# Decode-step transformer block on one core: the first w_mod load issued as 16 rows and 112 rows

## The chip, the cores and the metric

The kernel runs on one core of one Trainium2 chip. The metric is the device time of one execution in microseconds. TensorE (PE), VectorE (DVE), ScalarE (ACT) and GpSimd (POOL) compute; SyncE (SP) issues all DMA transfers of this kernel from one queue, and 16 DMA engines carry them out.

## What is computed

Two sequences with one new token each (B = 2, D = 512) go through an adaptive-layernorm block. The condition c gives six vectors per sequence, which scale, shift and gate an attention over the last 4096 positions of a cache (32 query heads on 8 key/value heads of 128) and a SiLU feed-forward of width 1792. All is float32.

```python
mod = (_silu(c) @ w_mod).reshape(c.shape[0], 6, 1, -1)
sa, ca, ga, sb, cb, gb = (mod[:, i] for i in range(6))
h = _layernorm(x) * (1 + ca) + sa
x = x + ga * attention(h, k_cache[:, :, -4096:], v_cache[:, :, -4096:], wq, wo)
h = _layernorm(x) * (1 + cb) + sb
x = x + gb * (_silu(h @ w1) @ w2)
```

Almost all bytes are read once: 64 MB of keys and values, and the weights w_mod (512 x 3072), wq (512 x 4096), wo (4096 x 512), w1 and w2.

## The kernel before, in words

Every large input is loaded in pieces of 128 rows into a ring of eight buffers of 128 x 4096 floats (`ring`, L55; `stream`, L69). A piece may be loaded when the piece eight places before it in the ring has been used. All loads are issued by SyncE in program order: `load_rows` (L72) for w_mod and wq, `load_k` and `load_v` (L77, L84) for the cache, `load_runs` (L91) for wo, w1 and w2. Each DMA signals its end on one of eight semaphores, taken in turn.

The program begins with the loads. L103 loads rows 0 to 127 of w_mod (`wm0`, 128 x 3072), then L107 loads c and x, each in two DMAs of small pieces, into `c_ch` and `x_ch`, which VectorE has cleared (L102). L111 loads the three other pieces of w_mod (`wm1` to `wm3`), L112 the four of wq. The loads of k and v follow in the loop over the heads.

Meanwhile VectorE and GpSimd build constants (L115 to L195): an identity and small selection matrices. VectorE transposes c (L235), its SiLU is made (L203 to L206, L238), and TensorE multiplies it with the pieces of w_mod (L246, L249). From the result and the normalised x comes `hq_T` (L263), the input of the q matmuls over the four pieces of wq (L285). The loop (L448) then takes one key/value head after the other: transposes of the keys on VectorE (L337), scores (L349), softmax, and the weighted sum of the values (L423). The tail multiplies with wo (L550, L561), does the second layernorm and the feed-forward (L595, L631, L643), and stores the output (L656).

The order of the instructions on each engine is a scheduler's, except in the loop and the tail, where `inorder` keeps the program's order. The operations of the beginning, those of VectorE among them, have no such mark.

Of the kernel before, what the change touches and what calls it, by code (L numbers as in the profile page):

```python
# [13 lines left out]
P = 128  # L14
B, D = 2, 512
# [8 lines left out]
def adaln_block(  # L24
# [21 lines left out]
    nc = tc.nc  # L46
# [22 lines left out]
    def stream(name):  # L69
        return ring.tile([P, 4096], F32, tag="st", name=name)  # L70

    def load_rows(name, w, k, width):  # L72
        t = stream(f"{name}{k}")[:, :width]
        nc.sync.dma_start(t, w[k * P : (k + 1) * P, :])
        return t
# [24 lines left out]
    x_sp, x_ch, c_ch = const([P, P], "x_sp"), const([P, P], "x_ch"), const([P, P], "c_ch")  # L100
    for t in (c_ch, x_ch, x_sp):
        nc.vector.memset(t, 0.0)  # L102
    wm = [load_rows("wm", w_mod, 0, 6 * D)]  # L103
    rows8 = lambda t: t.rearrange("(ab r) m -> ab r m", r=16)[:, 0, :]
    for t, src in ((c_ch, c), (x_ch, x2)):
        for b in range(B):
# [577 lines left out]
```

## Time and profile before

| | us |
|---|---|
| three runs: median (lowest, highest) | 237.36 (237.23, 237.38) |
| the profiled execution: its own time | 236.89 |
| the profiled execution: span from first to last instruction | 235.0 |

The profile describes the one profiled execution; times in it count from the span's start. A page gives busy times per engine, DMA queues and the chain of work that ended last. A window row gives, for a stretch A:B, its length, then for PE, PEld (weight loads), DVE, ACT and POOL the busy time in us and the number of instructions, then the granted TensorE clock, the mean busy share of the 16 DMA engines and the GB/s that they moved; a packet is counted where it starts, so a share can be above 1. A timeline row gives start, duration, engine (SPq is SyncE's issuing of DMAs), line, operation, tiles and, in brackets, how long the engine had been idle and what ended that. A row of the chain of waits gives start, duration and what the end was waiting for.

### The profile page before, as it was taken

How to read it: one execution, taken by the hardware profiler on the slowest of the kernel's cores; microseconds unless marked ns; L12 is line 12 of the kernel's file. 1: busy time of each engine (PE TensorE's matmuls, PEld its weight loads, DVE VectorE, ACT ScalarE, POOL GpSimd, SP SyncE). 2: the span in 40 equal slices, each digit the busy share in tenths (PEclk: the TensorE clock that was granted, in tenths of full speed). 3: DMA queues.
4: the chain of work that ended last, by engine and by line, in shares of the span. 5: the costliest groups of instructions: out<-in, count | busy, mean ns of one | idle time of the engine just before them, and what ended most of it. 6: DMA issues, size and time to landing. Idle time of an engine off the chain costs nothing.

```text
span 235.0 us, 2644 instructions
## 1 busy us (share of the span) xinstructions
PE 146.5 (62%) x1094; PEld 45.9 (20%) x1094; DVE 114.6 (49%) x176; ACT 25.4 (11%) x56; POOL 10.3 (4%) x30
## 2 busy tenths in 40 slices
PE   0086546367187577667549519626743967788993
PEld 0032101101011121121112102111211222335332
DVE  0634000793694792693892792595298050002130
ACT  2200000100300200200200200200020021003210
POOL 8600000100000000000000000000000000000000
PEclk9999975759869997999976967965985799999999
DMA  6999999999999999999999999999999999999991
GB/s 253 426 438 427 427 438 427 424 439 427 429 441 424 427 438 427 429 438 424 429 435 429 427 432 432 432 429 432 428 429 429 429 432 429 432 426 422 421 412 56
DMA packets 7603, 97.69 MB, mean 416 GB/s; under 512 B 920, under 2 KB 936, under 8 KB 1576
## 3 DMA queue, kind: packets, MB, share of 16 engines
q1 hardware_dynamic: 7592, 97.54, 97.5%
q8 instruction: 8, 0.13, 0.2%
q14 instruction: 3, 0.02, 0.0%
HBM read 97.53 MB, written 0.00 MB: 415 GB/s over the span
## 4 chain that ended last, share of the span: by engine, by line
DMA 64%; DVE 22%; PE 10%; ACT 2%; issue 1%; SPq 1%; DVEq 0%
DVE kT L337 16%; DMA wo<-in_A_wo_dram 14%; DMA k<-in_A_k_cache_dram 14%; DMA v<-in_A_v_cache_dram 13%; DMA wq<-in_A_wq_dram 13%; DMA w<-in_B_w_dram 7%; PE s L349 5%; DMA wm<-in_w_mod_dram 3%; DVE zp L395 2%; PE o L423 2%; PE q L285 1%; DVE xp L393 1%; ACT pr L381 1%; DVE mx L359 1%; ACT L381 1%
## 5 line engine op out<-in xcount | busy, mean ns | idle before, releaser
L337 DVE STREAM_TRANSPOSE kT<-k 128x1024 f32<-128x1024 f32 x64 | 73.7, 1210 | 1.6 <-DMA k<-in_A_k_cache_dram 1.6
L349 PE MATMUL s<-kT,qbd 128*32 128x512 f32 x256 | 44.5, 670 | 11.2 <-DVE kT L337 11.1
L423 PE MATMUL o<-v,ptb 128*32 128x512 f32 x256 | 38.5, 730 | 19.8 <-DMA v<-in_A_v_cache_dram 19.3
L359 DVE TENSOR_REDUCE mx<-s 128x1 f32<-128x512 f32 x8 | 5.5, 691 | 40.1 <-PE s L349 40.1
L349 PEld LDWEIGHTS s<-kT,qbd 128*32 128x32 f32 x256 | 11.1, 126 | 45.8 <-issue 24.1
L285 PE MATMUL q<-wq,hq_T 128*32 128x512 f32 x64 | 11.2, 836 | 10.1 <-DMA wq<-in_A_wq_dram 10.1
L423 PEld LDWEIGHTS o<-v,ptb 128*32 128x32 f32 x256 | 8.1, 124 | 35.8 <-issue 33.1
L402 PE MATMUL pT<-zp,id 128*32 128x256 f32 x64 | 5.6, 418 | 13.9 <-DVE zp L395 13.9
L379 ACT COPY bias<-bp 128x1 f32<-128x1 f32 x8 | 1.3, 159 | 111.9 <-PE bp L377 111.9
L537 PE MATMUL junk<-selh,id 128*32 128x256 f32 x46 | 11.3, 380 | 0.0
L294 DVE STREAM_TRANSPOSE qT<-q 128x512 f32<-128x512 f32 x2 | 1.4, 718 | 18.6 <-PE q L285 18.3
L395 DVE TENSOR_TENSOR zp<-xp,group 128x1024 f32<-128x1024 f32 x8 | 9.8, 1225 | 0.2
L393 DVE STREAM_TRANSPOSE xp<-pr 128x512 f32<-128x512 f32 x8 | 5.6, 701 | 4.4 <-ACT pr L381 4.4
L217 PE MATMUL mean_a<-mv_a,avg 128*128 128x1 f32 x2 | 0.6, 362 | 10.6 <-DVE mv_a L214 10.6
L361 PE MATMUL mT<-ident,mx 128*1 128x128 f32 x16 | 3.0, 270 | 6.4 <-DVE mx L359 6.4
L550 PE MATMUL acc_o<-wo,oTn 128*32 128x512 f32 x48 | 5.8, 598 | 1.9 <-DMA wo<-in_A_wo_dram 1.6
L537 PEld LDWEIGHTS junk<-selh,id 128*32 128x32 f32 x46 | 5.0, 110 | 6.7 <-issue 3.5
L438 PE MATMUL o_all<-ob,selh 128*64 128x128 f32 x64 | 5.7, 304 | 0.8 <-ACT ob L432 0.8
L270 DVE STREAM_TRANSPOSE xT<-x_sp 128x128 f32<-128x128 f32 x1 | 0.4, 403 | 11.8 <-DMA x_sp<-in_A_x_dram 11.8
L432 ACT COPY ob<-o 128x512 f32<-128x512 f32 x8 | 4.7, 585 | 10.3 <-PE o L423 10.3
L285 PEld LDWEIGHTS q<-wq,hq_T 128*32 128x32 f32 x64 | 2.1, 128 | 18.8 <-DMA wq<-in_A_wq_dram 12.5
L249 PE MATMUL m_sp<-wm,scT 128*32 128x512 f32 x32 | 5.7, 796 | 0.0
(132 smaller groups left out, 95.0 us busy)
## 6 DMA issues: line engine op xcount, KB each, us to landing
k<-in_A_k_cache_dram SPq DMA_DIRECT2D x16, 2048.0 KB, 30.2
v<-in_A_v_cache_dram SPq DMA_DIRECT2D x16, 2048.0 KB, 31.5
wq<-in_A_wq_dram SPq DMA_DIRECT2D x4, 2048.0 KB
wo<-in_A_wo_dram SPq DMA_DIRECT2D x4, 2048.0 KB, 32.3
wm<-in_w_mod_dram SPq DMA_DIRECT2D x4, 1536.0 KB, 10.2
w<-in_B_w_dram SPq DMA_DIRECT2D x2, 1024.0 KB, 23.2
w<-in_B_w_dram SPq DMA_DIRECT2D x1, 1792.0 KB
w<-in_B_w_dram SPq DMA_DIRECT2D x2, 896.0 KB
```

The lines of the kernel that those rows point to most:

```text
L249: nc.tensor.matmul(m_sp[r, :], scT[:, k, :], cd[:, g], start=(k == 0), stop=(k == 3))
L285: nc.tensor.matmul(q_ps[n][32 * g : 32 * g + 32, :], hq_T[:, k, :], wv[:, n, g], start=(k == 0), stop=(k == 3),)
L337: inorder(nc.vector.transpose(kT[h, b][:, :, 8 * n4 : 8 * n4 + 8, :].rearrange("p j n k -> p n j k"), kt[h, b][:, n4 * 1024 : (n4 + 1) * 1 ...
L349: inorder(nc.tensor.matmul(s_ps[h][r : r + 32, :], qbd[h // 4][:, h % 4, b, j, :], kT[h, b][:, j, 16 * c : 16 * c + 16, :], start=(j == 0) ...
L359: inorder(nc.vector.tensor_reduce(mx, s_ps[h], axis=AX.X, op=ALU.max))
L393: inorder(nc.vector.transpose(xp, pr[h]))
L395: inorder(nc.vector.tensor_mul(zp, xp[:, None, :, 0:16].to_broadcast([P, 4, 16, 16]), group[:, :, None, None].to_broadcast([P, 4, 16, 16]),))
L402: inorder(nc.tensor.matmul(tp[32 * i : 32 * i + 32, :], id4, zp.rearrange("p a s x -> p (a s) x")[:, :, 4 * i : 4 * i + 4], start=True, st ...
L423: inorder(nc.tensor.matmul(o_ps[h][32 * c : 32 * c + 32, :], ptb[h % 2][:, 256 * b + 32 * w : 256 * b + 32 * w + 32], vt[h, b][:, 512 * w ...
L438: inorder(nc.tensor.matmul(o_all[r : r + 64, :], selh[:, m, HQ - G - G * h : 3 * HQ - G - G * h], o_sb[h][:, m * DH : (m + 1) * DH], start ...
L537: inorder(nc.tensor.matmul(junk[0:32, :256], id4, selh.rearrange("p m y -> p (m y)")[:, :256], start=True, stop=True,))
L550: inorder(nc.tensor.matmul(acc[32 * g : 32 * g + 32, :], oTn[:, q, :], wot[q // 8][:, q % 8, :], start=(q < 4), stop=(q >= 20),))
```

## The change

The load of rows 0 to 127 of w_mod is issued as two DMAs into the same buffer, rows 0 to 15 first and rows 16 to 127 second. Both are ahead of the loads of c and x, as the one DMA was. All else in the source is the same; lines behind the change have numbers that are higher by four.

```diff
-    wm = [load_rows("wm", w_mod, 0, 6 * D)]
+
+    wm0 = stream("wm0")[:, : 6 * D]
+    for p0, p1 in ((0, 16), (16, P)):
+        nc.sync.dma_start(wm0[p0:p1, :], w_mod[p0:p1, :])
+    wm = [wm0]
     rows8 = lambda t: t.rearrange("(ab r) m -> ab r m", r=16)[:, 0, :]
     for t, src in ((c_ch, c), (x_ch, x2)):
         for b in range(B):
```

In the built program SyncE has one DMA more, and two VectorE instructions, the transpose of c (L235) and the first step of its SiLU (L203), stand behind the set-up operations on the identity, which they preceded. The instructions of the other engines stand as they did.

## The prediction

> **What bounds the kernel now.** I read the page first, for the share of each engine and the row of the DMA queue:
>
> ```profile
> span 235.0 us, 2644 instructions
> PE 146.5 (62%) x1094; PEld 45.9 (20%) x1094; DVE 114.6 (49%) x176; ACT 25.4 (11%) x56; POOL 10.3 (4%) x30
> ...
> q1 hardware_dynamic: 7592, 97.54, 97.5%
> ```
>
> No computing engine is busy for more than 62% of the span, while the packets of the one queue that SyncE feeds fill 97.5% of it. To see whether that queue ever runs dry, and where it starts and stops, I then cut the span into windows (the last two columns are the mean busy share of the 16 DMA engines, and GB/s):
>
> ```profile
> 0.00:1.50 1.50, 0.00 (x0) 0.00 (x0) 0.50 (x5) 0.77 (x1) 0.89 (x7) 1.00 0.00 0
> 1.50:2.00 0.50, 0.00 (x0) 0.00 (x0) 0.00 (x0) 0.50 (x1) 0.50 (x2) 1.00 1.55 270
> 2.00:2.50 0.50, 0.00 (x0) 0.00 (x0) 0.00 (x0) 0.02 (x1) 0.50 (x4) 1.00 0.20 49
> 2.50:3.00 0.50, 0.00 (x0) 0.00 (x0) 0.00 (x0) 0.00 (x0) 0.50 (x3) 1.00 0.63 221
> 3.00:3.50 0.50, 0.00 (x0) 0.00 (x0) 0.00 (x0) 0.00 (x0) 0.50 (x2) 1.00 0.98 418
> ...
> 4.00:228.00 224.00, 143.02 (x1034) 44.18 (x1035) 113.52 (x169) 23.55 (x54) 6.91 (x16) 0.86 1.01 430
> ...
> 228.50:229.00 0.50, 0.50 (x4) 0.22 (x2) 0.00 (x0) 0.38 (x1) 0.00 (x0) 1.00 0.92 369
> 229.00:229.50 0.50, 0.48 (x7) 0.17 (x9) 0.00 (x0) 0.21 (x1) 0.00 (x0) 1.00 0.77 311
> ```
>
> From 4 to 228 us the DMA engines are busy all the time (1.01; packets are counted where they start) at 430 GB/s. So the kernel is one stream of bytes: nothing before 1.5 us, a ragged first 1.5 us, 224 us at full rate, and a tail. The chain of waits, in order of time, shows what follows the last byte:
>
> ```profile
> 0.73 6.16 DMA wm<-in_w_mod_dram
> ...
> 213.97 16.51 DMA w<-in_B_w_dram
> 230.48 0.04 issue
> 230.53 1.10 PE acc_y L643 x24
> ```
>
> After the last weights land at 230.48 us comes a fixed end of 4.5 us up to the span's 235.0. Hence the rule for this kernel: a microsecond lost or won at the head of the stream is lost or won at the end, because no later gap takes it up. The change touches just that head.
>
> For later use: 430 GB/s over 16 engines that are busy 1.01 of the time is 26.6 GB/s for each, so one row of w_mod (3072 floats, 12,288 bytes) takes an engine 0.46 us.
>
> **The change part by part.** The profiled execution took 236.89 us, 1.89 outside its span; the median shown is 237.36, 0.47 more. I work out a difference from the profiled execution and add it to the median.
>
> *One more DMA on SyncE's queue.* The rows of that queue:
>
> ```profile
> 0.73 0.40 SPq L74 DMA_DIRECT2D wm<-in_w_mod_dram  x1
> 1.19 1.29 SPq L107 DMA_DIRECT2D c_ch<-in_c_dram  x2
> 2.53 1.09 SPq L107 DMA_DIRECT2D x_ch<-in_A_x_dram  x2
> 3.65 1.40 SPq L74 DMA_DIRECT2D wm<-in_w_mod_dram  x3
> 6.91 1.81 SPq L74 DMA_DIRECT2D wq<-in_A_wq_dram  x4
> 16.14 5.23 SPq L79 DMA_DIRECT2D k<-in_A_k_cache_dram  x4
> ...
> 181.60 0.58 SPq L474 DMA_DIRECT2D x_sp<-in_A_x_dram  x1
> 7.09 0.31 DVE L235 STREAM_TRANSPOSE cT<-c_ch 128x128 f32<-128x128 f32 x1 [5.75 <-DMA c_ch<-in_c_dram]
> ```
>
> A load of wm costs SyncE 0.40 us at the front and 1.40 / 3 = 0.47 later. The second part therefore pushes the loads of c, of x and of wm1 to wm3 back by some 0.45 us. In time this costs nothing: wm1 would be issued at 4.1 instead of 3.65, while the bytes of wm0 keep the engines occupied until its landing at 0.73 + 6.16 = 6.89 us, and c, which stands in line behind wm0, is seen by VectorE at 7.09. Without that cover the price would be 0.45 us. Each part has a semaphore of its own out of eight that go round, so behind it every user shifts by one: the load of wm3 now waits for the 16 rows and that of wq0 for the 112 (in the kernel before, wq0 waits for the whole of wm0: hence the jump to 6.91). The 16 rows are long there when SyncE comes to wm3 at about 5 us, and wq0 is no later than now. Behind them every load waits for the eighth before it, as now. Costed at nothing; if the 16 rows landed past 5 us, only wm3 and the wq loads queue behind the wait, with two loads of 3.7 us in stock.
>
> *VectorE's order.* In the order of instructions the transpose L235 and L203 that follows it now stand behind the nine set-up operations of which these are the first and the last but one:
>
> ```profile
> 7.32 0.33 DVE L118 TENSOR_REDUCE id<-ident 128x32 f32<-128x128 f32 x1
> ...
> 9.72 0.17 DVE L156 COPY selh<-id 128x32 f32<-128x32 f32 x1
> ...
> 13.29 1.08 PE L246 MATMUL m_ch<-wm,scT 128*32 128x256 f32 x8 [0.86 <-DVE scT L238]
> ...
> 22.99 1.93 PE L285 MATMUL q<-wq,hq_T 128*32 128x512 f32 x16 [2.02 <-DMA wq<-in_A_wq_dram]
> ...
> 39.01 1.94 PE L285 MATMUL q<-wq,hq_T 128*32 128x512 f32 x8 [2.06 <-DMA wq<-in_A_wq_dram]
> ```
>
> So the set-up from 7.32 to 9.8 us is done while VectorE waits for c, and the first modulation matmul may start up to 2.5 us before 13.29. That gain is hidden: the q matmuls wait for wq anyway, from 22.99 to 39.01, and the k loads that wm's freed buffers allow (16.14) stand in a queue that is full. Nothing for the time; it is cover against a later wm0.
>
> *How the stream starts.* The 0.1 us windows show the first packets:
>
> ```profile
> 1.60:1.70 0.10, 0.00 (x0) 0.00 (x0) 0.00 (x0) 0.10 (x1) 0.10 (x2) 1.00 0.00 0
> 1.70:1.80 0.10, 0.00 (x0) 0.00 (x0) 0.00 (x0) 0.10 (x1) 0.10 (x1) 1.00 3.48 614
> ```
>
> They start at 1.7. By 3.0 us, 0.5 x (270 + 49 + 221) = 270 KB have been started, where 430 GB/s from 1.7 on would have made 559. So at most 289 KB / 430 = 0.67 us is there to be won at the head. An earlier first packet isn't to be had: the load of x_sp, eight rows, took SyncE 0.58 us to issue, no less than 128 rows did. Part of the 0.67 can come if a short first load sets all engines going together, where now 11 packets (135 KB) start in 1.5 to 2.0 us and 2 in the next half microsecond. But the second part is issued 0.45 us later than those rows are now. Bounds: -0.67 to +0.45. I take half the gain, **-0.33 us**.
>
> *The 16 rows themselves.* All big loads here have 128 rows; none shows what a 16-row load does, whose rows lie in 16 neighbouring partitions. From below: all 16 engines abreast, one row each, 0.46 us, no loss. From above: each row behind the other, 16 x 0.46 = 7.4 us. The nearest row is the first window: 0.5 us x 16 x 1.55 = 12.4 engine-us on 11 packets, 1.13 us each, so that even rows spread over 128 partitions take 2.4 times their price at the start. Neighbours can only be worse: I take the geometric middle of the bounds, four row times, 1.85 us, a loss of 1.85 - 0.46 = **+1.39 us**.
>
> [...]
>
> *The 112 rows.* Each engine has 7 rows where it had 8. If they are dealt out as evenly as 128 rows are, no loss; if all go as the 16 do, 7 x 1.39 = +9.7 us. Since the 112 span nearly the partitions of the 128 rows, which run at full rate, I stay near that end with one row time, **+0.46 us**, and up to three (+1.39) for the range.
>
> **Sum:** -0.33 + 1.39 + 0.46 = +1.52 us, 237.36 + 1.52 = **238.9 us**; on the profiled execution 238.4.
>
> **The rivals.** About 0.2% (0.47 us, from 236.89 to 237.83) is what a measurement can tell from no change.
>
> *The rows do not obstruct each other.* Then only the start counts: half its gain, or the second part late by up to 0.45 us: 237.0 to 237.8, likeliest **237.2**. For it: the stream runs at 430 GB/s however the 16 engines' rows fall. Against: that is shown for 128 rows alone.
>
> *Faster: a clean start.* With no obstruction and no late second part the ragged head closes, -0.67 us: **236.7**. It decides if more than 0.47 of the 0.67 us comes back, that is if by 3.0 us over 470 KB have been started in place of 270. For it: the hole at 2.0 to 2.5 us (49 GB/s). Against: the later second part, and that first packets of 1.13 us look slow on their own account.
>
> *The 112 rows obstruct throughout:* +1.39 + 9.7 - 0.33, about **248**.
>
> *It doesn't change the head,* since both parts queue on the same engines at once: this is the first rival's time.
>
> **How the numbers follow.** Forecast (obstruction at the head) 0.47, no obstruction 0.35, clean start 0.14, obstruction throughout 0.04. From the last and the forecast comes slower, 0.51; same 0.35; faster 0.14. The forecast's own range is from +0.47 to +1.39 + 1.39 = 2.78 us, 237.8 to 240.1. Since both signs are likely, the range for all reaches down over the no-obstruction case, **237.0 to 240.1**, and leaves out the clean start and the 248.
>
> **What would show it.** In the profile after, windows of 0.5 us: by the forecast the stream gets to 418 GB/s only past 4.5 us, with shares near 1 at low GB/s (packets of 1.8 us) before; without obstruction the 2.0 to 3.0 windows are as now or fuller. The load of wm0 should land near 8.4 us (6.89 + 1.52), the set-up of VectorE should stand before it, and the first q matmul, last byte and end should all be later by the same amount. If the head is later and the end isn't, my rule that the stream has no gap is wrong; if the head looks the same and the end moves, the cause lies in the windows behind 4 us, and I have missed it.

## The result and the profile after

The changed kernel takes **238.71 us** (median of 6 runs, 238.61 to 239.04) against 237.26 (6 runs, 237.10 to 237.38): slower by 1.45 us, ratio 1.0063, 95% interval 1.005 to 1.0076. The forecast was 238.9. The time is right; two of the terms behind it are not, and that their errors cancel is luck.

The page of the profile after, first its span and the row of the DMA queue:

```profile
span 236.8 us, 2645 instructions
...
q1 hardware_dynamic: 7608, 97.54, 97.6%
```

The same 97.54 MB, 16 packets more, and a span that is 1.8 us longer; the profiled execution took 238.66 us, 1.77 more than that of before. Where that lies is seen from windows. First the kernel before, in five stretches (last column GB/s):

```profile
1.50:3.00 1.50, 0.00 (x0) 0.00 (x0) 0.00 (x0) 0.52 (x1) 1.50 (x7) 1.00 0.80 180
3.00:4.00 1.00, 0.00 (x0) 0.00 (x0) 0.00 (x0) 0.00 (x0) 1.00 (x4) 1.00 1.01 430
4.00:8.00 4.00, 0.00 (x0) 0.00 (x0) 0.91 (x5) 0.00 (x0) 4.00 (x9) 1.00 1.02 420
8.00:9.00 1.00, 0.00 (x0) 0.00 (x0) 1.00 (x2) 0.00 (x0) 1.00 (x3) 1.00 1.03 430
9.00:228.00 219.00, 143.02 (x1034) 44.18 (x1035) 111.61 (x166) 23.55 (x54) 1.91 (x7) 0.86 1.01 430
```

and the same stretches after:

```profile
1.50:3.00 1.50, 0.00 (x0) 0.00 (x0) 1.31 (x6) 0.51 (x1) 1.50 (x6) 1.00 1.24 254
3.00:4.00 1.00, 0.00 (x0) 0.00 (x0) 0.79 (x5) 0.00 (x0) 1.00 (x4) 1.00 0.45 123
4.00:8.00 4.00, 0.00 (x0) 0.00 (x0) 0.00 (x0) 0.00 (x0) 4.00 (x8) 1.00 1.04 296
8.00:9.00 1.00, 0.00 (x0) 0.00 (x0) 0.00 (x0) 0.00 (x0) 1.00 (x3) 1.00 0.85 299
9.00:228.00 219.00, 144.52 (x1020) 44.55 (x1024) 111.11 (x160) 23.57 (x54) 2.01 (x7) 0.84 1.01 430
```

From 9 us on both run at 430 GB/s. Ahead of it the stream first gains 1.5 x (254 - 180) = 111 KB, which is 0.26 us at 430 GB/s; then it loses 430 - 123 = 307 KB (0.71 us) between 3 and 4, and 4 x (420 - 296) + (430 - 299) = 627 KB (1.46 us) between 4 and 9. In sum 1.91 us late, and that is the longer span (1.8). The stretch from 4 to 8 tells most: the engines are as busy as before (1.04), and the bytes are 30% fewer. Packets take longer (an estimated 0.69 us for 12,288 bytes, from 1.04 x 16 engines at 296 GB/s, in place of 0.46); nothing waits.

Nor do the engines stand idle between 3 and 4, though the share there is low (0.45). Windows of 0.5 us of the kernel after show it:

```profile
2.50:3.00 0.50, 0.00 (x0) 0.00 (x0) 0.50 (x3) 0.00 (x0) 0.50 (x2) 1.00 2.06 320
3.00:3.50 0.50, 0.00 (x0) 0.00 (x0) 0.50 (x4) 0.00 (x0) 0.50 (x2) 1.00 0.13 25
```

The first row holds 320 x 0.5 / 12.3 = 13 packets, which take 2.06 x 0.5 x 16 / 13 = 1.27 us each in place of 0.46. They are counted where they start and keep the engines until about 3.7 us.

The chain of waits in order of time (start, duration, what was waited for) carries it to the end:

```profile
1.19 7.90 DMA wm<-in_w_mod_dram
...
215.64 16.54 DMA w<-in_B_w_dram
232.18 0.04 issue
232.23 1.06 PE acc_y L647 x24
```

The 112 rows land at 9.09 us where the whole of wm0 landed at 6.89; the last weights land at 232.18 where they landed at 230.48, later by 1.70; the end behind them is as long as it was. The timeline after, for the steps of the prediction that were costed at nothing:

```profile
0.73 0.86 SPq L106 DMA_DIRECT2D wm<-in_w_mod_dram  x2
4.12 1.41 SPq L74 DMA_DIRECT2D wm<-in_w_mod_dram  x3
9.11 1.75 SPq L74 DMA_DIRECT2D wq<-in_A_wq_dram  x4
3.64 0.15 DVE L151 TENSOR_TENSOR selg<-selg,half 128x8 f32<-128x8 f32 x1
9.24 0.31 DVE L239 STREAM_TRANSPOSE cT<-c_ch 128x128 f32<-128x128 f32 x1 [5.44 <-DMA c_ch<-in_c_dram]
13.02 1.08 PE L250 MATMUL m_ch<-wm,scT 128*32 128x256 f32 x8 [0.86 <-DVE scT L242]
24.94 2.93 PE L289 MATMUL q<-wq,hq_T 128*32 128x512 f32 x16 [3.42 <-DMA wq<-in_A_wq_dram]
```

wm1 is issued 0.47 us later and still ahead of need, c comes 2.15 us later, and VectorE has done its set-up by then (the last of it at 3.64), so that the first modulation matmul starts at 13.02 and not behind 13.29. The q matmuls still wait for wq.

### The profile page after: what moved, and what is told of

The parts are those of the page before. It is cut to its first block, busy times and chain, and to the rows that moved or that the text cites. A ratio compares the mean times of both kernels' runs of the same rounds, so it can differ in the third digit from the quotient of the medians.

```text
span 236.8 us, 2645 instructions
## 1 busy us (share of the span) xinstructions
PE 149.6 (63%) x1094; PEld 46.7 (20%) x1094; DVE 114.3 (48%) x176; ACT 25.4 (11%) x56; POOL 10.4 (4%) x30
## 3 DMA queue, kind: packets, MB, share of 16 engines
q1 hardware_dynamic: 7608, 97.54, 97.6%
## 4 chain that ended last, share of the span: by engine, by line
DMA 63%; DVE 25%; PE 7%; ACT 2%; issue 1%; SPq 1%; POOL 0%; POOLq 0%
DMA k<-in_A_k_cache_dram 26%; DVE kT L341 18%; DMA wo<-in_A_wo_dram 14%; DMA wq<-in_A_wq_dram 13%; DMA w<-in_B_w_dram 7%; PE s L353 5%; DMA wm<-in_w_mod_dram 3%; DVE zp L399 3%; DVE xp L397 1%; ACT pr L385 1%; DVE mx L363 1%; DVE qT L298 1%; ACT L385 1%; SPq L74 1%; PE mT L365 0%
## 5 line engine op out<-in xcount | busy, mean ns | idle before, releaser
L427 PE MATMUL o<-v,ptb 128*32 128x512 f32 x256 | 40.1, 757 | 22.1 <-DMA v<-in_A_v_cache_dram 21.6
L353 PE MATMUL s<-kT,qbd 128*32 128x512 f32 x256 | 43.5, 675 | 9.3 <-DVE kT L341 9.3
L289 PE MATMUL q<-wq,hq_T 128*32 128x512 f32 x64 | 11.8, 873 | 9.3 <-DMA wq<-in_A_wq_dram 9.3
L554 PE MATMUL acc_o<-wo,oTn 128*32 128x512 f32 x48 | 7.3, 753 | 0.8 <-DMA wo<-in_A_wo_dram 0.5
```

The lines of the kernel that those rows point to most:

```text
L289: nc.tensor.matmul(q_ps[n][32 * g : 32 * g + 32, :], hq_T[:, k, :], wv[:, n, g], start=(k == 0), stop=(k == 3),)
L353: inorder(nc.tensor.matmul(s_ps[h][r : r + 32, :], qbd[h // 4][:, h % 4, b, j, :], kT[h, b][:, j, 16 * c : 16 * c + 16, :], start=(j == 0) ...
L427: inorder(nc.tensor.matmul(o_ps[h][32 * c : 32 * c + 32, :], ptb[h % 2][:, 256 * b + 32 * w : 256 * b + 32 * w + 32], vt[h, b][:, 512 * w ...
L554: inorder(nc.tensor.matmul(acc[32 * g : 32 * g + 32, :], oTn[:, q, :], wot[q // 8][:, q % 8, :], start=(q < 4), stop=(q >= 20),))
```

## The experiments

Three theories. **A:** a load of fewer than 128 neighbouring rows is slow, above all the 112, because its rows are dealt out unevenly or go to partitions that get in each other's way. **B:** any second DMA at the head starts late and cold. **C**, the prediction's largest term: it is the 16 rows. Some runs change only the load of wm0, at the head; others change the 16 k loads, in the middle of the stream. The edits are to the two lines of the changed kernel, or to the DMA of `load_k` in the kernel before, where `rows` is its source with 128 rows of 16,384 bytes.

**1. Two parts by columns.**

```diff
-    for p0, p1 in ((0, 16), (16, P)):
-        nc.sync.dma_start(wm0[p0:p1, :], w_mod[p0:p1, :])
+    for e0, e1 in ((0, 384), (384, 6 * D)):
+        nc.sync.dma_start(wm0[:, e0:e1], w_mod[0:P, e0:e1])
```

> The load of wm0 in two parts of 128 rows each: columns 0 to 383 first (196,608 bytes, as many as 16 rows), then 384 to 3071. Three theories. A: in the changed kernel the 112-row part is what is slow, because a load of less than 128 rows is dealt out unevenly; parts of 128 rows cost nothing, so this takes 237.0 to 237.3 us, and its packets after the first row run at the full rate. B: any second DMA at the head starts cold and late; this takes 238.5 to 238.9 us like the changed kernel. C (the prediction's): the 16 neighbouring rows obstruct each other; here there are none, 237.0 to 237.3 us as by A.

237.20 us against 237.13, ratio 1.0003 (0.9994 to 1.0011). Two DMAs with as many bytes each as in the change cost nothing when each has 128 rows: B is out as the cause of 1.45 us. Slow packets at the start are here too:

```profile
2.50:3.00 0.50, 0.00 (x0) 0.00 (x0) 0.00 (x0) 0.00 (x0) 0.50 (x3) 1.00 1.90 387
```

That is 0.97 us for each 12,288 bytes, against 1.27 in the changed kernel.

**2. The 112 rows first.**

```diff
+    for p0, p1 in ((0, 112), (112, P)):
```

> The load of wm0 as rows 0 to 111 first, then rows 112 to 127. A: the 112-row part alone costs some 2 us and has no short first load in front of it, 239 to 240 us, and the first seven rows of each engine take 5 us in the windows. B: the short part comes second with its issue hidden, 237.3 us. C: the cost moves with the 16 rows behind the 112, 238.6 us, and the windows are full until about 5 us.

239.69 us, ratio 1.0102 (1.0086 to 1.0118). As A has it, the loss starts with the 112 rows, now without a gain ahead. In the window from 4 to 8 us:

```profile
4.00:8.00 4.00, 0.00 (x0) 0.00 (x0) 0.00 (x0) 0.00 (x0) 4.00 (x8) 1.00 1.08 253
```

Not all of this is the 112 rows. Near the place where the 16 rows now stand in the queue (by count, the 124th to 135th of the large packets) packets are slowest, 1.28 us each, and there the stream has long been running:

```profile
7.00:8.00 1.00, 0.00 (x0) 0.00 (x0) 0.00 (x0) 0.00 (x0) 1.00 (x2) 1.00 0.99 152
```

So this run fits A's time, and it holds a loss near the 16 rows as well.

**3. Two halves.**

```diff
+    for p0, p1 in ((0, 64), (64, P)):
```

> The load of wm0 as rows 0 to 63 and 64 to 127. [...] B: one more DMA as in the changed kernel, 238.7 us. C: no 16-row load, 237.3 us.

240.25 us, ratio 1.0126 (1.0111 to 1.0142): 1.5 us above B's 238.7 and 3 us above C's 237.3. The rate is half of 420 and stays there:

```profile
4.00:8.00 4.00, 0.00 (x0) 0.00 (x0) 0.00 (x0) 0.00 (x0) 4.00 (x8) 1.00 0.99 209
8.00:9.00 1.00, 0.00 (x0) 0.00 (x0) 0.00 (x0) 0.00 (x0) 1.00 (x3) 1.00 0.97 197
```

There is no 16-row load here. C alone can't be the cause. That fits A, two loads of less than 128 neighbouring rows being slow; why it is a half the run doesn't show.

**4. The 16 rows alone.** They go into a spare buffer (one of the two key buffers, not in use yet), and wm0 is loaded whole behind them.

```diff
+    spare = ktp.tile([P, 4096], F32, tag="kT", name="spare")
+    nc.sync.dma_start(spare[0:16, : 6 * D], w_mod[0:16, :])
+    nc.sync.dma_start(wm0, w_mod[0:P, :])
```

> 16 rows of w_mod are loaded first into a spare buffer that nothing reads, then wm0 whole with 128 rows. One row time of 0.46 us more is moved per engine. A: the 16 rows are harmless and let the engines start together, so 237.3 + 0.46 - 0.35 = 237.4 us. B: a second DMA costs 1.4 + 0.46: 239.1 us. C: 1.39 + 0.46: 239.1 us or more.

237.75 us, +0.62 (ratio 1.0025, 1.0015 to 1.0034), of which 0.46 is the row time of the added bytes. A's figure is the nearer, though it had a start gain of 0.35 that isn't there. The windows show why:

```profile
1.50:3.00 1.50, 0.00 (x0) 0.00 (x0) 1.31 (x6) 0.51 (x1) 1.50 (x6) 1.00 1.27 262
3.00:4.00 1.00, 0.00 (x0) 0.00 (x0) 0.79 (x5) 0.00 (x0) 1.00 (x4) 1.00 0.36 147
4.00:8.00 4.00, 0.00 (x0) 0.00 (x0) 0.00 (x0) 0.00 (x0) 4.00 (x8) 1.00 0.98 411
```

The first two rows are those of the changed kernel (254, then 123): a gain up to 3 us and a dip behind it that takes back more than that. With 128 rows behind the 16 the rate is back at 411 by 4 us; with 112 it is 296. So of the change's 1.91 us the stretch to 4 us belongs to the short first load with whatever follows it, net 0.71 - 0.26 = +0.45, and the 1.46 behind it to the 112 rows. Some of the +0.45 came with the second load by columns too: that run had moved 616 KB at 4 us where the kernel before had moved 700, which is 0.20 us.

**5 to 7. The same splits in the stream, for all k loads.** Columns as control, then 16 and 112, then 64 and 64.

```diff
-            t, k_cache[b, h, SK - W :, :].rearrange("(p n) d -> p (n d)", p=P)
+        for e0, e1 in ((0, 512), (512, 4096)):            # control
+            nc.sync.dma_start(t[:, e0:e1], rows[:, e0:e1])
...
+        for p0, p1 in ((0, 16), (16, P)):                 # then ((0, 64), (64, P))
+            nc.sync.dma_start(t[p0:p1, :], rows[p0:p1, :])
```

> The kernel before, with each of the 16 k loads (2 MB, 128 rows of 16,384 bytes) issued in two parts by columns, 512 and 3584 wide, 128 rows each. It is the control for the next two: the same number of DMAs as they have. A: 237 to 238 us, only packets of 2 KB instead of one of 16 KB at the margin. B (a second DMA costs): if it costs only at the cold head, 237.3 too; if everywhere, up to 16 x 1.4 = 260 us.

238.67 us against 237.24, ratio 1.0056 (1.0033 to 1.0078): 1.4 us for 16 added DMAs and smaller packets, 0.1 each, a little above A's range; B, if it held everywhere, would have been 1.4 each.

> The kernel before, with each of the 16 k loads issued as rows 0 to 15 and 16 to 127, far from the head of the stream. A: the 112-row part costs some 2 us x 16,384/12,288 = 2.7 us each time, 280 us or more. B: the cost is one of the cold head, 237 to 238 us. C: only the 16 rows cost, 1.85 us each time, 267 us, and the rate dips are short.

337.5 and 356.7 us in two executions: 6.3 and 7.5 us for each k load, more than A's lower figure and far from both others. Each load has a part of 16 rows too, and by the faster execution of run 9 such a part costs 9.0 / 8 = 1.1 us. That leaves an estimated 5 us for the 112 rows, if the two add.

> The kernel before, with each of the 16 k loads issued as rows 0 to 63 and 64 to 127. [...] B and C: 237 to 238 us.

351.87 us, ratio 1.4832 (1.477 to 1.4894): 7.2 us for each k load, where half the rate, which the halves had at the head (209 GB/s), would be 4.9 more. The row of GB/s in the page's 40 slices:

```profile
GB/s 300 434 433 422 281 214 210 211 236 411 208 214 326 309 219 216 405 210 214 238 339 216 212 233 304 220 221 240 291 221 218 257 360 424 420 436 420 345 80 14
```

210 to 220 in the stretches of k loads is half of 430; the extra must lie in the loads between, since full rate comes back only now and then (405 to 411). The mean of a longer stretch agrees:

```profile
40.00:200.00 160.00, 66.55 (x384) 18.07 (x384) 62.34 (x73) 10.84 (x28) 0.95 (x4) 0.65 1.01 255
```

k loads at 215 GB/s and as many bytes of v at 430 would make an estimated 287, and it is 255 at full busy share. Why the other loads suffer was not tried.

**8. Same source, other partitions.** Each half of the cache rows is read as in the kernel before this one, but written to every second partition.

```diff
+        spread = t.rearrange("(i j) x -> j i x", j=2)
+        for j in range(2):
+            nc.sync.dma_start(spread[j], rows[64 * j : 64 * j + 64, :])
```

> Each k load in two parts of 64 rows that read the same halves of the cache as the kernel with rows 0 to 63 and 64 to 127 (351.9 us), but write every second partition: the first part 0, 2, ... 126, the second 1, 3, ... 127. (Keys stand in other partitions than their values, so the attention's result is another one; the work is the same.) If the loss lies on the memory that is read, the time is the same, 352 us. If it lies in which partitions are written at a time, the time differs: 240 us if reaching all 128 partitions in one load is enough, something between if engines still meet in the same partitions.

**237.10 us**, ratio 0.9998 (0.9987 to 1.0009): none of the 114 us is left.

```profile
GB/s 249 424 433 432 435 421 435 435 425 429 437 424 432 432 426 432 435 426 429 432 432 426 432 428 432 432 429 432 432 426 429 432 429 432 430 426 425 419 413 58
```

This is the run that decides. The number of DMAs, the rows of each and what is read are the same; only the partitions written differ. So the loss of the halves lies in which partitions a load writes, and 64 rows as such cost nothing. The 112 rows were not spread in this way.

**9 and 10. Sixteen rows in the stream,** neighbours, and every eighth partition, from the same source.

```diff
+        for j in range(8):
+            nc.sync.dma_start(t[16 * j : 16 * j + 16, :], rows[16 * j : 16 * j + 16, :])
...
+        spread = t.rearrange("(i j) x -> j i x", j=8)
+        for j in range(8):
+            nc.sync.dma_start(spread[j], rows[16 * j : 16 * j + 16, :])
```

> Each k load in eight parts of 16 neighbouring rows. C (the prediction's term): four row times per part, 8 x 4 x 0.611 = 19.6 us per k load instead of 4.9, 237 + 16 x 14.7 = 472 us. A (whatever is less than 128 rows runs at half rate, as the 64 and 112 did): 237 + 16 x 4.9 to 7.1 = 315 to 351 us. If 16 rows are harmless, as the head of the changed kernel looked: 237 to 245 us.

> The same eight parts of 16 rows of the cache, each written to every eighth partition (0, 8, ... 120, then 1, 9, ...) instead of to neighbours. (Keys stand in other partitions than their values; the work is the same.) If the side that is read sets the price, the same time as with neighbours; if the partitions that are written set it, clearly less.

Neighbours: 381.7 and 435.4 us, 9 to 12 us for each k load. That is between A's 351 and C's 472: in a full stream 16 neighbours are the worst of all, and four row times are not far off. The GB/s of the longer execution:

```profile
GB/s 322 432 431 254 135 132 136 132 133 266 236 139 141 312 219 133 122 340 174 113 136 263 236 109 121 178 331 122 121 165 339 130 127 121 376 428 426 428 422 134
```

Every eighth partition: 334.4 us, ratio 1.4109 (1.4027 to 1.4191), clearly less from the same source. Its stretches are near 210:

```profile
GB/s 294 431 431 434 314 217 219 204 219 340 312 211 221 398 233 154 221 411 243 211 284 365 164 188 259 407 164 217 288 370 168 229 330 421 438 431 422 424 419 69
```

So there are three levels: about 430 GB/s for 128 rows or every second partition, about 215 for 64 neighbours or 16 rows at every eighth partition, about 130 for 16 neighbours (in the longer of its two executions).

**11 and 12. Back to the head, with spread partitions.** wm0 in two parts of every second row, and in four parts of every fourth; the second is the attempt at a version that keeps a short first load and loses nothing.

```diff
+    spread = lambda t: t.rearrange("(i j) m -> j i m", j=2)    # then j=4
+    for j in range(2):                                         # then range(4)
+        nc.sync.dma_start(spread(wm0)[j], spread(w_mod[0:P, :])[j])
```

> wm0 in two parts of 64 rows, every second row (0, 2, ... and 1, 3, ...), each row to its own partition. If the partitions that one load reaches set its rate, this goes without the loss of rows 0 to 63 and 64 to 127 (240.25 us): 237.0 to 237.3 us. If something else at the head made that loss, 239 us or more.

237.50 us against 236.92, ratio 1.0023 (1.0014 to 1.0032): 2.5 us less over its own reference than with halves (+0.58 against +3.12), yet above what was expected.

```profile
1.50:3.00 1.50, 0.00 (x0) 0.00 (x0) 1.30 (x6) 0.52 (x1) 1.50 (x6) 1.00 0.70 131
3.00:4.00 1.00, 0.00 (x0) 0.00 (x0) 0.80 (x5) 0.00 (x0) 1.00 (x4) 1.00 0.93 319
4.00:8.00 4.00, 0.00 (x0) 0.00 (x0) 0.71 (x3) 0.00 (x0) 4.00 (x8) 1.00 1.01 420
```

From 4 us the rate is that of before. The 0.5 us is lost ahead of it: nothing moves before 2 us here (0 GB/s from 1.5 to 2.0 us, 270 in the kernel before). SyncE needed 1.23 us to issue these two loads, 0.86 for the two of the change.

> wm0 in four parts of 32 rows, every fourth row. It keeps what the change has, a short first load, and avoids neighbouring partitions. If a short first load wins part of the ragged head (up to 0.67 us by the prediction's bound), 236.6 to 237.0 us, below both kernels; if the packets that follow are late by as much, 237.1 to 237.4; if 32 rows also obstruct, 238 us or more.

239.66 us (238.14 to 240.11), ratio 1.0098 (1.0072 to 1.0125): slower, against the expectation. Its profiled execution was one of the short ones, 238.14. SyncE's queue and two windows of it:

```profile
0.73 2.48 SPq L107 DMA_DIRECT2D wm<-in_w_mod_dram  x4
3.26 1.29 SPq L112 DMA_DIRECT2D c_ch<-in_c_dram  x2
4.59 1.08 SPq L112 DMA_DIRECT2D x_ch<-in_A_x_dram  x2
5.72 1.39 SPq L74 DMA_DIRECT2D wm<-in_w_mod_dram  x3
```

```profile
6.00:6.50 0.50, 0.00 (x0) 0.00 (x0) 0.00 (x0) 0.00 (x0) 0.50 (x4) 1.00 1.20 492
6.50:7.00 0.50, 0.00 (x0) 0.00 (x0) 0.00 (x0) 0.00 (x0) 0.50 (x1) 1.00 0.90 202
7.00:7.50 0.50, 0.00 (x0) 0.00 (x0) 0.00 (x0) 0.00 (x0) 0.50 (x2) 1.00 0.91 204
7.50:8.00 0.50, 0.00 (x0) 0.00 (x0) 0.00 (x0) 0.00 (x0) 0.50 (x1) 1.00 0.47 152
```

Four issues instead of one push wm1 from 3.65 to 5.72 us, and wm0's bytes no longer cover that: behind 6.5 us the rate falls to 200 and less for 1.5 us, with packets of 0.88 us (0.90 x 8 us over 8.2 packets from 6.5 to 7.0). It looks as if the stream had run dry and started as slowly as at the head. This is argued from the windows; whether it is the same in the executions of 239.4 to 240.1 us wasn't seen. No version here beats the kernel before.

## Why the prediction was right, and where it was wrong

*The rule that the head passes to the end: right.* 1.91 us late at 9 us, 1.70 at the last weights, 1.8 in the span.

*SyncE's queue, costed at nothing for the cover of wm0's bytes: right,* and the four-part version shows the price once the cover is gone (wm1 issued at 5.72 us, 202 and 204 GB/s between 6.5 and 7.5). wq0 came later only because the 112 rows landed later.

*VectorE's order, costed at nothing: right.* It hid a c that came 2.15 us later.

*The start, -0.33: half right.* The gain up to 3 us was 0.26. The loss behind it, 0.71, is above the bound of +0.45 that the prediction set for a late second part, and it isn't lateness: the engines are held by packets of 1.27 us. So the short first load came to +0.45 net and not to a gain.

*The 16 rows, +1.39: too large at this place.* Loaded ahead of a whole wm0 they cost 0.62 - 0.46 = 0.16 us. The mechanism exists: k loads in parts of 16 neighbours lose 9 to 12 us per 2 MB, where four row times would be 14.7, and packets of 1.27 us follow the 16 rows at the head. There most of the price is probably hidden, for the kernel before loses up to 0.67 us in its ragged start at the same place. How much of the slow packets belongs to the 16 rows and how much to the start (0.97 us with columns) the runs don't separate.

*The 112 rows, +0.46: mis-sized, and this is the step that failed.* The prediction argued that 112 rows span nearly the partitions of 128 and stayed near that end. They cost 1.46 us behind 4 us: 296 GB/s, where 128 rows behind the same 16 ran at 411. In the stream they cost an estimated 5 us per 2 MB, nearer to the 7.2 of the halves than to nothing. Nearly all partitions is not the point. The prediction's words "if they are dealt out as evenly as 128 rows are" held the right question; which engine writes which of the 112 rows the trace doesn't show, and it stays open. It shows only that an added DMA brings 16 packets more in both splits (with 16 added DMAs 7,848 packets, 16 and 112 as 64 and 64, where the kernel before has 7,592).

*The sum* came out at +1.52 against +1.45 because one term was too large and the other too small, by about a microsecond each: its nearness is luck. The prediction had the full rate back past 4.5 us, and it came at about 9. Both terms stood for one mechanism, loads whose rows obstruct each other. The runs confirm it for 64 neighbours (351.87 us against 237.10 with the same rows spread) and for 16 (381.7 and 435.4 against 334.4); that it is the same for the 112 is the author's estimate and not shown.

## What to carry to other kernels

Where a stream of loads is the bound, keep each load on all 128 partitions and split it, if at all, by columns or by every second partition: 16 split loads cost 1.4 us by columns, nothing by every second partition, and 100 us or more by neighbours. A load's price is read from a window at full busy share, much longer than a packet: share near 1 with fewer GB/s (1.04 and 296 from 4 to 8 us, 1.02 and 420 before the change) came from slow packets here, and from neither issue nor waits. A right total does not prove its terms; the part done alone does.

## What the runs showed of the hardware that was not expected

- 64 rows to every second partition run at the full 430 GB/s, 64 rows to neighbours at 210 to 220.
- 112 neighbouring rows are far from free: 296 GB/s at the head, where 128 rows behind the same short load ran at 411.
- SyncE took 0.43 us to issue a part of 16 or 112 rows of wm0 (0.86 for two), and 0.62 for one of 32 rows (2.48 for four) or of every second row (1.23 for two).
- A short first load does not shorten the head: up to 3 us more bytes are started (254 against 180 GB/s), and the next microsecond gives back more than that (123 against 430).
